# Spacing the background pieces behind the last big first-layer tile by TensorE time

## The chip, the cores and the metric

The kernel runs on one core of a Trainium2 chip. The metric is the device time of one execution in microseconds (us), the median of several runs; lower is better. The engines are TensorE (PE in the profile, PEld its weight loads), VectorE (DVE), ScalarE (ACT), GpSimd (POOL) and SyncE (SP, which issues the transfers).

## The reference

Three parts follow each other: windowed attention, a routed expert layer with a gate, and a second expert layer in which every expert takes exactly `N // E` tokens.

```
x = attention(q, k, v)                       # 3072 tokens x 512
e_idx = argmax(x @ w_gate + bias[modality])  # first layer: each token to its best expert
x = gate_w * (relu(x @ w1[e]) @ w2[e])
logits = x @ w_gate2                         # second layer: greedy, at most cap = 384 tokens for each expert
for idx in argsort(-logits.flatten()):
    tok, e = idx // E, idx % E
    if free(tok) and counts[e] < cap: assign(tok, e)
out = relu(x[assigned to e] @ w21[e]) @ w22[e]
```

The routing of the second layer needs the second gate's logits of every token, so it can begin in full only when the last tile of the first layer has been computed.

## The kernel before

The first expert layer (`moe1`) runs eight tiles through `Ffn.run`: six big ones of 512 tokens (four blocks of 128) and two small ones of 128 tokens, numbered 0 to 7 here. A tile has eight steps, and the loop has steps 0 to 69. In a step, the first part is the first matmul of one slice of weights (`ph`, L871 for a small tile, L928 for a big one), the second part is the second matmul (`y`, L871) of an earlier slice: two steps back for a big tile, six for a small one. Every matmul is done three times, with high and low parts of both operands (`w1h`, `w1l`, `w2h`, `w2l`, `hh`, `hl`); ACT rounds a slice of weights to its high part and DVE subtracts to get the low part, two steps ahead. Steps 48 to 63 make the first parts of the two small tiles; steps 50 to 53 have no second part, and steps 64 to 69 no first part. A small tile's `hr` is transposed on PE after each fourth slice.

Each step has four ticks (`side(0)` to `side(3)`: behind the first part, behind that, behind the second part's first block, at the end of the step). A tick issues a part of the weights' rounding, sometimes a transposition of the next tile's tokens (`xprep`, into the one PSUM bank `tr`), and then calls the hook, which takes pieces from the background queue `BG` in their order and issues them. The order of the instructions on each engine is thereby written out by hand: an engine works through them in that order.

When a block's second matmul is done, `yout` copies it to `yr` on ACT and adds pieces to the queue. For the last big tile and the small ones these are `put` (a store to `xs`), `turn` (four transposes on PE into `tr`, and a copy to `yt` on ACT), `logits` (four fp32 matmuls on PE into the bank `rt`) and `keep` (DVE copies the logits out; for a small tile it also prepares its part of the search). Behind the last block of the last big tile come the fifteen pieces of `Route.pre`, which prepare the search for the first expert of the second layer: b1 to b6 (bounds of the logits), v1 to v3 (best expert and comparison, DVE), p1 (13 small matmuls, PE), v4 (DVE), p2 (one matmul, PE), v5, v6, v7 (DVE). Pieces that do nothing (`nop`) stand between them; a tick takes one piece, or two when more than twelve wait. `late_ids` of the second small tile is added in step 54. What is left when the loop ends is issued by `bg.drain()`, and then `moe2` begins with the first count of its search (L1410 into `rt`).

`Clock` is a count kept while the program is built: `clk.pe` grows by 1/2400 us for each column that TensorE gets. The second layer's routing (`Route.steps`) is placed by it. In the first layer `clk.mm` is called for the matmuls and the transposes of tokens and of `hr`, but not for `turn` and `logits`.

Of the kernel before, what the change touches and what calls it, by code (L numbers as in the profile page):

```python
# [66 lines left out]
class K:  # L67
    def __init__(self):
        self.clk = Clock()
# [82 lines left out]


class BG:
    def __init__(self):
        self.q = []

    def add(self, *fs):
        self.q.extend(fs)

    def pop(self, n=1):
        for _ in range(n):
            if self.q:
                self.q.pop(0)()

    def drain(self):
        while self.q:
            self.q.pop(0)()


LST, LPV, LRO = 3, 2, 4
# [812 lines left out]
class Src:  # L984
# [15 lines left out]
    wait = 0  # L1000
# [7 lines left out]
    pop = idle  # L1008


class Src1(Src):

    wait = 12
# [29 lines left out]

    def force_e(self, j):
        while not self.ready_e(j):
            self.G.bg.pop(1)

    def force_x(self, j):
        while not self.ready_x(j):
            self.G.bg.pop(1)  # L1050

    def entry(self, w, j):
        return self.G.etab[0:1, w, j:j + 1] if j < NE else self.G.tab[0:1, w, j - NE:j - NE + 1]
# [97 lines left out]
def moe1(tc, g, G, src, rt, w1, w2, wg2, wg2T):  # L1151
    nc = tc.nc
    with ExitStack() as ctx:
        ctx.enter_context(tc.manual_schedule())
        f = Ffn(ctx, tc, g, "m1", tpe=TPE, rawpool=src.pool, vsplit=True)
        g.pst = lambda: f.ps.tile([128, 512], F32, name="rt")
        bg = G.bg
        wgb = gate_rows(nc, f, wg2T)
        wgc = f.wk.tile([128, 4, E], F32, name="wgc", bufs=1)
        nc.sync.dma_start(wgc, wg2.rearrange("(c p) e -> p c e", p=128))  # L1160
        nop = lambda: None
        bank = lambda: f.ps.tile([128, 512], F32, name="y1")
        static = list(range(SBIG)) + list(range(NE + NBIG, NE + NBIG + SSML))
        V = nc.vector

        def yout(j, a, y):
            c = src.first(j)
            late = c - NMAIN
            yr = f.wk.tile([128, DM], F32, name=f"yr{(a + max(late, 0)) % 4}", bufs=1)
            lg = rt.LG[:, c + a]  # L1170
            nc.scalar.activation(yr, y, AF.Copy, scale=src.gate(j, a))
            st = {}

            def turn():
                p = f.ps.tile([128, 512], F32, name="tr", bufs=f.trbufs)
                for c in range(4):
                    nc.tensor.transpose(p[:, 128 * c:128 * c + 128], yr[:, 128 * c:128 * c + 128], g.ident)
                st["t"] = f.wk.tile([128, 4, 128], F32, name="yt")
                nc.scalar.activation(st["t"], p, AF.Copy)
                if j == static[-1]:  # L1180
                    f.warm(WT[5])

            def logits():
                st["p"] = f.ps.tile([128, 512], F32, name="rt")[:, 0:E]
                for c in range(4):
                    nc.tensor.matmul(st["p"], st["t"][:, c, :], wgc[:, c, :], start=(c == 0), stop=(c == 3))
                if j == static[-1]:
                    f.warm(WT[6])

            def keep():  # L1190
                if late >= 0:
                    rt.keep(late, st["p"])
                V.tensor_copy(lg, st["p"])

            def put():
                nc.sync.dma_start(rt.xs[128 * (c + a):128 * (c + a) + 128, :], yr)

            if j in static[:-3]:
                bg.add(put, *dots(nc, f, yr, wgb, lg))
            else:  # L1200
                bg.add(nop, put, nop, turn, nop, nop, nop, logits, nop, keep)
                if j == static[SBIG - 1] and a == src.width(j) - 1:
                    bg.add(*rt.pre(bank, 1))

        def onx(j, xg):
            if j == static[SBIG - 1]:
                bg.add(*rt.main_ids())
            elif j in static[SBIG:]:
                bg.add(*rt.late_ids(static.index(j) - SBIG))
            if j == static[-1]:  # L1210
                nc.gpsimd.drain()

        f.run(static, w1, w2, src, yout, hook=lambda: bg.pop(2 if len(bg.q) > 12 else 1), pre=(src.raw, dict(src.xg)),
              onx=onx, LEAD=2)
        bg.drain()

# [6 lines left out]
XO = 9  # L1223
X0 = 2.0
SC = 6
PW = 4, 3, 3
WT = 7, 2, 6, 3, 6, 4, 8, 16, 0, 2
BIG = 3.0e38
BG1 = 1.0e37
# [67 lines left out]
class Route(Src):  # L1297
# [115 lines left out]
    def pre(self, bank, wait):  # L1413


        nc, g, p = self.nc, self.g, self.p
        V = nc.vector
        both, main = slice(0, 2), slice(0, HT)
        mb = bank()
        pn, pb2, pv = (self.views(mb)[i] for i in (1, 5, 6))  # L1420
        pb2 = pb2.rearrange("p (a e) -> p a e", a=2)
        bs, pd = self.bounds(V, mb, "a")
        dd0 = p.tile([128, 2, NIT], F32, name="dd0")
        gg = p.tile([JC, 2, E], BF, name="gg2")
        gs = p.tile([JC, E], F32, name="gs")
        J8 = p.tile([128, E], F32, name="J8")
        L = self.L

        def b5():
            V.tensor_scalar(self.lo0, pd[:, 1:2], -1.0, None, op0=OP.mult)  # L1430
            V.tensor_tensor(self.span, pd[:, 0:1], self.lo0, op=OP.subtract)
            self.sizes(V, pd)

        def b6():
            V.tensor_scalar(self.J, self.nrow, 4.0, None, op0=OP.mult)
            V.tensor_scalar(self.fl, g.iota[:, 0:E], 1.0, self.J, op0=OP.add, op1=OP.mult)
            self.widths(V, dd0, 0, self.span)
            V.tensor_scalar(self.lop, dd0[:, 0, 0:1], -128.0, self.lo0, op0=OP.mult, op1=OP.add)

        def v1():  # L1440
            V.tensor_copy(fold(L)[:, both, HT + 1:HR], bc(self.fl[:, None, None, :], [128, 2, HR - HT - 1, E]))
            Lm = fold(L)[:, both, main]
            V.tensor_tensor(Lm, self.LG[:, 0:NMAIN].rearrange("p (a t) e -> p a t e", a=2),
                            bc(self.pn.rearrange("p (a t) -> p a t", a=2)[:, :, :, None], [128, 2, HT, E]), op=OP.add)
            V.tensor_tensor(Lm, Lm, bc(self.fl[:, None, None, :], [128, 2, HT, E]), op=OP.max)

        def v2():
            self.best(V, both, main)

        def v3():  # L1450
            self.compare(V, both, main, dd0[:, 1, 0:1])

        def p1():
            nc.tensor.matmul(pv, g.ones, self.vb, start=True, stop=True, skip_group_check=True)
            self.count(pn, range(HT))

        def v4():
            V.tensor_copy(gs, pn[JC:2 * JC, E:2 * E])
            V.tensor_tensor(gs, pn[0:JC, 0:E], gs, op=OP.add)
            V.tensor_reduce(self.nv, pv, axis=AX.X, op=OP.add)  # L1460
            V.tensor_scalar(self.nv, self.nv, float(CAP) - 0.5 - N, None, op0=OP.add)
            V.tensor_scalar(gg[:, 0], gs, float(CAP) - 0.5, None, op0=OP.is_ge)
            V.tensor_scalar(gg[:, 1], gs, self.nv[0:JC], None, op0=OP.is_ge)

        def p2():
            nc.tensor.matmul(pb2, g.ones[0:JC, :], gg, start=True, stop=True, skip_group_check=True)

        def v5():
            d = dd0[:, 0, 0:1]
            V.max(J8, pb2[:, 0])  # L1470
            V.tensor_reduce(self.J2, pb2[:, 1], axis=AX.X, op=OP.max)
            V.tensor_scalar(self.b0, d, -1.5, self.lo0, op0=OP.mult, op1=OP.add)
            V.scalar_tensor_tensor(self.lo, J8[:, 0:1], d, self.b0, op0=OP.mult, op1=OP.add)
            V.tensor_scalar(self.lb, J8, d, self.b0, op0=OP.mult, op1=OP.add)
            V.scalar_tensor_tensor(self.hi, self.J2, d, self.b0, op0=OP.mult, op1=OP.add)
            V.tensor_tensor(self.hi, self.hi, d, op=OP.add)

        def v6():
            V.tensor_tensor(self.span, self.hi, self.lo, op=OP.subtract)
            self.widths(V, self.dd1, 1, self.span)  # L1480
            V.tensor_scalar(self.lop, self.dd1[:, 0, 1:2], -128.0, self.lo, op0=OP.mult, op1=OP.add)

        def v7():
            self.compare(V, both, main, self.dd1[:, 1, 1:2])
        nop = [lambda: None] * wait
        q = []
        for f in bs + [b5]:
            q += [f] + nop
        q.append(b6)
        for f in (v1, v2, v3, p1, v4, p2, v5):  # L1490
            q += nop * (PW[0] if f in (p1, p2) else 1) + [f]
        return q + nop * PW[1] + [v6] + nop * PW[2] + [v7]

    def digits(self, ids, o):

# [401 lines left out]
def tile_kernel(ctx, tc, qT, kT, v4, vsT, vsR, mid, wg, mbias, w1, w2, wg2, wg2T, w21, w22, cst, out):  # L1897
    nc = tc.nc
    g = K()
# [1 line left out]
    xs = tc.dram_tile([NSL + 1, DM], F32, name="xs")  # L1901
    cp = ctx.enter_context(tc.tile_pool(name="cst", bufs=1))
    load_consts(nc, g, cp, cst)
    bg = BG()
    rp = ctx.enter_context(tc.tile_pool(name="m2r", bufs=1))
    rt = Route(nc, g, rp, xs)
    with ExitStack() as c1:
        gp = c1.enter_context(tc.tile_pool(name="gate", bufs=1))
        pre = c1.enter_context(tc.tile_pool(name="pre", bufs=2))
# [51 lines left out]
```

## Time and profile before

| | us |
|---|---|
| median of three runs | 918.66 |
| the three runs | 915.5, 918.66, 920.61 |
| profiled execution, own time | 923.71 |
| its span | 922.0 |
| PE busy | 859.1 |
| DVE busy | 635.0 |
| ACT busy | 407.7 |

The profiled execution is one more run of the same program, with the profiler on; its span goes from the first to the last instruction. A busy time is the sum of an engine's instructions in that span. Times of the trace are microseconds from the start of the span. "The granted clock" is the share of full speed at which TensorE was let run.

### The profile page before, as it was taken

Reading aid. Unit: us, or ns where it says so; the run is one execution under the profiler, and the core shown is the slowest. Engines: PE = TensorE matmul, PEld = TensorE weight load, DVE = VectorE, ACT = ScalarE, POOL = GpSimd, SP = SyncE. Lnnn points to the kernel's source line nnn. Section 1 sums busy time; section 2 is a strip of 40 time slices with the busy share of each in tenths; the row PEclk is TensorE's granted clock in tenths of the full one; section 3 lists DMA queues with packets and bytes.
Section 4 is the critical chain, followed back from the end, with each engine's and each line's share of the span. In section 5 each row is a group of like instructions: output and inputs, shape, how many; then the busy total and the mean of one; then the engine's idle time right before and its main releaser. Section 6 shows DMA issues by size and latency. Waiting matters only on the chain.

```text
span 922.0 us, 15329 instructions
## 1 busy us (share of the span) xinstructions
PE 859.1 (93%) x5035; PEld 682.6 (74%) x5040; DVE 635.0 (69%) x1815; ACT 407.7 (44%) x1135; POOL 352.9 (38%) x555
## 2 busy tenths in 40 slices
PE   8789898998999999999997887989899999999996
PEld 4556666666888888888886545778788787889995
DVE  3878688866869696969783958777868676733220
ACT  3677677763343333333335514233334233334441
POOL 2785647583311010100000005536363546555561
PEclk9999899999999999999999999999999799999999
DMA  8244555376444444444344215325353425345301
GB/s 253 93 139 139 127 152 138 106 235 229 92 160 128 147 134 141 138 138 130 115 152 155 100 48 181 121 98 174 123 168 110 135 72 177 105 142 190 115 35 39
DMA packets 68944, 123.92 MB, mean 134 GB/s; under 512 B 9075, under 2 KB 21365, under 8 KB 68726
## 3 DMA queue, kind: packets, MB, share of 16 engines
q1 hardware_dynamic: 62166, 103.41, 35.3%
q0 software_dynamic: 6688, 19.43, 6.4%
q8 instruction: 42, 0.69, 0.3%
q14 instruction: 48, 0.39, 0.2%
HBM read 103.11 MB, written 19.71 MB: 133 GB/s over the span
## 4 chain that ended last, share of the span: by engine, by line
PE 70%; DVE 15%; issue 5%; ACT 5%; POOL 3%; DMA 2%; SPq 0%; POOLq 0%; ACTq 0%; DVEq 0%
PE y L871 26%; PE ph L928 26%; PE sp L296 3%; ACT P L325 3%; PE rt L1410 2%; DVE sc L150 2%; PE tr L740 2%; PE po L368 2%; PE rc L1273 1%; DVE mx L315 1%; DVE cmp L150 1%; PE pt L333 1%; PE px L403 1%; DMA vsx<-in_vsR_dram 1%; PE y L749 1%
## 5 line engine op out<-in xcount | busy, mean ns | idle before, releaser
L937 ACT ACTIVATE hh<-ph 128x384 fp32r<-128x384 f32 (+1 forms) x112 | 60.2, 537 | 269.6 <-PE ph L928 269.0
L928 PE MATMUL ph<-xh,w1h 128*128 128x384 f32 (+1 forms) x448 | 171.6, 383 | 0.0
L871 PE MATMUL y<-w2h,hh 128*128 128x512 f32 x400 | 164.7, 412 | 0.0
L928 PE MATMUL ph<-xh,w1l 128*128 128x384 f32 (+1 forms) x448 | 163.9, 366 | 0.0
L928 PE MATMUL ph<-xl,w1h 128*128 128x384 f32 (+1 forms) x448 | 162.6, 365 | 0.0
L871 PE MATMUL y<-w2l,hh 128*128 128x512 f32 x400 | 159.6, 399 | 0.0
L871 PE MATMUL y<-w2h,hl 128*128 128x512 f32 x400 | 159.5, 399 | 0.0
L938 DVE SCALAR_TENSOR_TENSOR hl<-ph,hh 128x384 fp32r<-128x384 f32 (+1 forms) x112 | 68.5, 612 | 112.9 <-ACT hh L937 112.7
L824 POOL TENSOR_TENSOR w2l<-w2r,w2h 128x512 fp32r<-128x512 f32 x64 | 89.8, 1410 | 62.1 <-ACT w2h L820 33.5
L1083 POOL DMA_INDIRECT xg<-xd,ent x26 | 30.5, 1172 | 214.0 <-PE tr L740 111.5
L1107 DVE SCALAR_TENSOR_TENSOR junk<-yr,wgb 128x512 f32<-128x512 f32 x160 | 103.4, 686 | 0.0
L928 PEld LDWEIGHTS ph<-xh,w1h 128*128 128x128 f32 x448 | 86.8, 194 | 10.4
L928 PEld LDWEIGHTS ph<-xh,w1l 128*128 128x128 f32 x448 | 86.5, 193 | 9.7
L325 ACT ACTIVATE P<-sp,mx 128x132 f32<-128x132 f32 x192 | 69.1, 367 | 54.4 <-DVE mx L315 31.8
L928 PEld LDWEIGHTS ph<-xl,w1h 128*128 128x128 f32 x448 | 86.0, 192 | 7.8
L871 PEld LDWEIGHTS y<-w2h,hl 128*128 128x128 f32 x400 | 76.7, 192 | 17.2 <-DVE hl L976 0.4
L871 PEld LDWEIGHTS y<-w2h,hh 128*128 128x128 f32 x400 | 77.2, 193 | 12.9 <-ACT hh L975 0.4
L871 PEld LDWEIGHTS y<-w2l,hh 128*128 128x128 f32 x400 | 77.1, 193 | 12.2 <-DVE w2l L824 0.3
L843 DVE TENSOR_TENSOR w1l<-w1r,w1h 128x512 fp32r<-128x512 f32 x96 | 74.3, 774 | 13.4 <-ACT w1h L838 13.4
L838 ACT ACTIVATE w1h<-w1r 128x512 fp32r<-128x512 f32 x128 | 79.7, 623 | 5.5 <-DMA w1r<-in_w_dram 3.2
L820 ACT ACTIVATE w2h<-w2r 128x512 fp32r<-128x512 f32 x128 | 79.4, 624 | 2.7 <-issue 2.5
L296 PE MATMUL sp<-kr,qs 64*128 64x260 f32 (+1 forms) x384 | 59.8, 409 | 18.8 <-ACT P L325 17.3
(343 smaller groups left out, 1442.3 us busy)
## 6 DMA issues: line engine op xcount, KB each, us to landing
w1r<-in_w_dram SPq DMA_DIRECT2D x32, 1024.0 KB, 5.4
w2r<-in_w_dram SPq DMA_DIRECT2D x32, 1024.0 KB, 6.4
xs<-yr SPq DMA_DIRECT2D x26, 256.0 KB, 6.0
kr<-in_kT_dram SPq DMA_DIRECT2D x16, 396.0 KB, 4.0
qr<-in_qT_dram SPq DMA_DIRECT2D x16, 384.0 KB, 3.3
vr<-in_v_dram SPq DMA_DIRECT2D x16, 384.0 KB, 4.5
xd<-xb SPq DMA_DIRECT2D x16, 384.0 KB, 5.7
wgb<-in_wg2T_dram SPq DMA_DIRECT2D x1, 2048.0 KB
```

The lines of the kernel that those rows point to most:

```text
L296: nc.tensor.matmul(sp[:, hd, c0:260], qs[o:o + 64, 128 * i:128 * i + 128], kr[o:o + 64, k0:k0 + 260 - c0], start=True, stop=True)
L325: nc.scalar.activation(z.P[:, n % 2, hd, :], s.sp[:, hd, 128:260], AF.Exp, bias=s.mx[:, hd:hd + 1], accum_out=z.sm[:, n % 2, hd:hd + 1])
L820: nc.scalar.activation(ch[1][c][0], r[:, q, :], AF.Copy)
L824: eng.tensor_tensor(lo, r[:, q, :], h.bitcast(F32), op=OP.subtract)
L838: nc.scalar.activation(h, v, AF.Copy)
L843: eng.tensor_tensor(lo, v, h.bitcast(F32), op=OP.subtract)
L871: nc.tensor.matmul(o, l, r, start=(first and i == 0), stop=(end and i == 2))
L928: nc.tensor.matmul(ph, wp[:, c, :], xp_[:, c, 0:NTK], start=(d == 0 and i == 0), stop=(d == 3 and i == len(cut[d]) - 1))
L937: nc.scalar.activation(hh, ph, AF.Relu)
L938: nc.vector.scalar_tensor_tensor(hl, ph, 0.0, hh.bitcast(F32), op0=OP.max, op1=OP.subtract)
L1083: self.nc.gpsimd.indirect_dma_start(out=self.xg[j][:, a, :], out_offset=None, in_=self.G.xd[0:k, :], in_offset=bass.IndirectOffsetOnAxis(a ...
L1107: nc.vector.scalar_tensor_tensor(junk, yr[:, 0:DM], 1.0, wgb[:, e, :], op0=OP.mult, op1=OP.mult, accum_out=lg[:, e:e + 1])
```

## The change

The queue's pieces may now carry a wait: a tuple `(us, piece)` is issued only when `clk.pe` has grown by at least so much since the last piece was issued. The hook tries two pieces in a tick when a tuple stands first. `drain` and the forced pops issue without regard to waits. `turn` and `logits` add their columns to the clock. The four blocks of the last big tile are interleaved: a block's `logits` is issued together with the next block's `turn`. The `nop` pieces behind that tile and in `Route.pre` are gone; the pieces carry waits in their stead.

```diff
 class BG:
-    def __init__(self):
-        self.q = []
+    def __init__(self, clk):
+        self.q, self.clk, self.last = [], clk, 0.0
...
-    def pop(self, n=1):
+    def pop(self, n=1, force=False):
         for _ in range(n):
             if self.q:
-                self.q.pop(0)()
+                f = self.q[0]
+                if isinstance(f, tuple):
+                    wait, f = f
+                    if not force and self.clk.pe < self.last + wait:
+                        return
+                self.q.pop(0)
+                f()
+                self.last = self.clk.pe
 
     def drain(self):
         while self.q:
-            self.q.pop(0)()
+            self.pop(1, True)
...
             def turn():
+                g.clk.mm(1080)
...
             def logits():
+                g.clk.mm(2100)
...
-                bg.add(nop, put, nop, turn, nop, nop, nop, logits, nop, keep)
+                bg.add((0.3, put))
+                if a > 0:
+                    prev = held.pop()
+                    bg.add((TL, prev[0]), turn, (0.4, prev[1]))
+                else:
+                    bg.add((1.0, turn))
+                held.append((logits, keep))
+                if a == src.width(j) - 1:
+                    bg.add((TL, logits), (0.4, keep))
...
-        f.run(static, w1, w2, src, yout, hook=lambda: bg.pop(2 if len(bg.q) > 12 else 1), pre=(src.raw, dict(src.xg)),
+        f.run(static, w1, w2, src, yout, hook=lambda: bg.pop(2 if len(bg.q) > 12 or bg.q and isinstance(bg.q[0], tuple) else 1), pre=(src.raw, dict(src.xg)),
...
-PW = 4, 3, 3
+TL = 1.8
...
-        q = []
-        for f in bs + [b5]:
-            q += [f] + nop
-        q.append(b6)
-        for f in (v1, v2, v3, p1, v4, p2, v5):
-            q += nop * (PW[0] if f in (p1, p2) else 1) + [f]
-        return q + nop * PW[1] + [v6] + nop * PW[2] + [v7]
+        b1, b2, b3, b4 = bs
+        return [b1, (2.0, b2), (0.5, b3), (1.6, b4), (0.5, b5), b6, (0.5, v1), (0.5, v2), (0.5, v3), (3.2, p1), (1.2, v4),
+                (2.0, p2), (0.4, v5), (0.6, v6), (0.6, v7)]
```

## Rows read from the trace of the kernel before

**Rows 1.** The page: busy time of the engines; the chain by engine.

```profile
PE 859.1 (93%) x5035; PEld 682.6 (74%) x5040; DVE 635.0 (69%) x1815; ACT 407.7 (44%) x1135; POOL 352.9 (38%) x555
...
PE 70%; DVE 15%; issue 5%; ACT 5%; POOL 3%; DMA 2%; SPq 0%; POOLq 0%; ACTq 0%; DVEq 0%
```

**Rows 2.** Windows of the loop's tail, middle, end: length; busy time; clock; DMA share; GB/s.

```profile
487.69:532.73 45.04, 35.71 (x188) 26.89 (x186) 31.37 (x96) 24.97 (x48) 0.00 (x0) 0.96 0.36 121
500.17:521.73 21.56, 15.82 (x76) 11.67 (x75) 17.32 (x61) 10.18 (x21) 0.00 (x0) 0.92 0.34 114
532.73:537.88 5.15, 4.26 (x24) 2.51 (x25) 1.12 (x6) 1.28 (x2) 0.00 (x0) 1.00 0.15 54
```

**Rows 3.** Waits from 486 to 538, TensorE's own: us, times, longest.

```profile
PE y L1410 <- DVE cmp L1404: 2.7, 1, 2.7
...
PE ph L871 <- DVE w1l L843: 1.6, 2, 1.4
...
PE rt L1186 <- ACT yt L1179: 1.4, 2, 0.7
PE y L1375 <- DVE mm L1372: 1.4, 1, 1.4
...
PE y L1382 <- DVE d L1379: 1.1, 1, 1.1
...
PE tr L972 <- ACT yt L1179: 0.7, 1, 0.7
```

**Rows 4.** Windows of 2 us around falls of the granted clock.

```profile
506.00:508.00 2.00, 2.00 (x6) 1.51 (x6) 0.58 (x4) 0.94 (x3) 0.00 (x0) 0.50 0.62 145
544.00:546.00 2.00, 1.13 (x15) 0.92 (x15) 1.07 (x3) 0.00 (x0) 0.00 (x0) 1.00 0.00 0
546.00:548.00 2.00, 2.00 (x7) 0.69 (x6) 1.61 (x11) 0.00 (x0) 0.00 (x0) 0.55 0.00 0
```

**Rows 5.** The chain of work around 485: start, us, what.

```profile
481.73 2.72 PE y L871 x12
...
488.53 0.45 PE tr L1177 x4
```

**Rows 6.** Timeline of TensorE: p1; `logits` of the last tile; the warming matmuls.

```profile
513.05 0.89 PE L1410 MATMUL y<-OH,cmp 128*128 128x16 bf16 x12 [2.67 <-DVE cmp L1404]
...
535.04 1.05 PE L1186 MATMUL rt<-wgc,yt 128*128 128x8 f32 x8
...
535.94 1.89 PE L749 MATMUL y<-wz 128*128 128x512 bf16 x8
```

**Rows 7.** Groups by line, DVE and ACT, 487.7 to 533: busy us, mean ns, idle before.

```profile
L824 DVE TENSOR_TENSOR w2l<-w2r,w2h 128x512 fp32r<-128x512 f32 x16 | 10.8, 685 | 0.0
...
L976 DVE TENSOR_TENSOR hl<-tr,hh 128x512 fp32r<-128x512 f32 x4 | 2.7, 687 | 3.2 <-ACT hh L975 3.2
...
L838 ACT ACTIVATE w1h<-w1r 128x512 fp32r<-128x512 f32 x12 | 7.5, 623 | 0.0
```

**Rows 8.** Windows of single pieces on DVE: b6+v1, v2+v3, v4, v5, v6, v7, digits, `keep`.

```profile
508.94:510.45 1.51, 1.44 (x10) 0.94 (x8) 1.41 (x9) 0.76 (x2) 0.00 (x0) 1.00 0.71 274
511.05:512.91 1.86, 0.00 (x0) 0.00 (x0) 1.79 (x5) 1.31 (x3) 0.00 (x0) 1.00 0.01 4
514.83:515.64 0.81, 0.61 (x3) 0.27 (x2) 0.74 (x6) 0.63 (x1) 0.00 (x0) 1.00 0.00 0
516.85:517.88 1.03, 1.03 (x6) 0.82 (x6) 0.96 (x9) 0.26 (x1) 0.00 (x0) 1.00 0.00 0
519.09:519.73 0.64, 0.64 (x5) 0.51 (x4) 0.57 (x5) 0.64 (x2) 0.00 (x0) 1.00 0.00 0
520.93:522.14 1.21, 1.19 (x6) 0.63 (x4) 1.21 (x4) 0.93 (x3) 0.00 (x0) 1.00 0.86 318
523.34:523.90 0.56, 0.42 (x2) 0.38 (x3) 0.56 (x8) 0.31 (x1) 0.00 (x0) 1.00 0.95 358
526.88:528.03 1.15, 1.15 (x6) 0.94 (x6) 1.05 (x7) 0.38 (x1) 0.00 (x0) 1.00 0.00 0
```

More of the change, by code (lines that the diff above doesn't have):

```diff
@@ L1045, in force_e @@
         while not self.ready_e(j):
-            self.G.bg.pop(1)
+            self.G.bg.pop(1, True)
     def force_x(self, j):
         while not self.ready_x(j):
-            self.G.bg.pop(1)
+            self.G.bg.pop(1, True)
     def entry(self, w, j):
@@ L1162, in moe1 @@
         bank = lambda: f.ps.tile([128, 512], F32, name="y1")
+        held = []
         static = list(range(SBIG)) + list(range(NE + NBIG, NE + NBIG + SSML))
@@ L1903, in tile_kernel @@
     load_consts(nc, g, cp, cst)
-    bg = BG()
+    bg = BG(g.clk)
     rp = ctx.enter_context(tc.tile_pool(name="m2r", bufs=1))
```

## The prediction

> **What bounds the kernel now.** I read the page first. PE is busy 93% of the span and carries 70% of the chain that ended last [rows 1], so what counts is time in which PE waits, and only where the change reaches. The windows over the tail of the first layer come next, from the end of the last big tile's second-layer matmuls (487.69) to the first count of the second routing (537.88) [rows 2]. The loop's steps 50 to 69 take 45.04 us and PE is busy in 35.71 of them; in the middle stretch DVE is busy 17.32 of 21.56 and the granted clock is 0.92. After the last matmul come 5.15 us up to the first count. The waits tell what PE lacked [rows 3]: 2.7 us for `cmp` of v3, 1.4 and 1.1 for `mm` and `d` of b1 and b3, 1.4 and 0.7 for `yt` of the blocks, and 1.6 for `w1l`, which stood on DVE behind the pieces of `pre`. That is 8.9 us. So the background pieces do cost time where they stand now, and about 9 us is what a better place could win at most from waits.
>
> **Where the pieces will stand.** The kernel's clock follows from its code: a small tile adds 1536 columns (0.64 us) in the first part of a step and 0.64 in the second; steps 50 to 53 have no second part, 64 to 69 no first; the transposes of `hr` add 0.43 in steps 52, 56, 60 and 64; `turn` now adds 0.45 and `logits` 0.88. Going through the ticks with the new waits gives: turn0 right behind the last big tile's matmuls (step 49), logits0 and turn1 in step 53, logits1 and turn2 in 56, logits2 and turn3 in 58, logits3 in 60, b1 in 60, b2 and b3 in 62, b4 in 64, b5 and b6 in 65, v1, v2, v3 in 66, 67, 68. p1 wants 3.2 after v3, and the loop has one step of 0.64 left. So p1, v4, p2, v5, v6, v7, the digits of tile 7's ids and all of tile 6's and tile 7's pieces fall to `bg.drain()`, behind the last matmul. Before, v7 came out in step 60, tile 6 was done in step 63, and only tile 7's `turn`, `logits` and `keep` were left. This is the heart of the forecast: the spacing is fit for the blocks, and too wide for what comes behind them.
>
> **The loop's gain.** From 45.04 us I take the 8.9 of waits [rows 3]: each `yt` now has over a step's work between `turn` and `logits`, b1 to b4 have steps between them, p1 is gone from the loop. I take 1.7 for the clock: 0.92 granted over 21.56 us is 8% lost, 1.7 us [rows 2], and the low stretch came just after b1 to b4 had made PE idle; where it fell, PE finished 6 matmuls in 2 us at 0.50 [rows 4]. I take 2.25 for PE work that leaves the loop: p1 0.89, p2 about 0.1, tile 6's `turn` 0.45 and `logits` 0.9 [rows 5, 6] (an estimate for p2, which is one small matmul). A full-speed matmul of 512 columns takes 2.72/12 = 0.227 us [rows 5], so the matmuls left are not changed.
>
> New waits I put at 5.8 us. Steps 50 to 53 hold only 0.69 us of matmuls each once the blocks are thinned out, while a slice of weights needs 0.62 on ACT and then 0.69 on DVE [rows 7]: `w1h` of step 52 stands on ACT behind three `yr` and `yt`, some 0.9 us late. In step 54 the one `tr` bank passes from turn1 to the next tile's transposes, whose `xh` stands on ACT behind `yt`, `w1h` and `w2h`: 1.1 us over four transposes. In steps 58 and 62 `hl` (0.69) stands ahead of `w1l` on DVE: 0.5 each, 0.3 elsewhere. That makes 3.3. At the end b5, b6 and v1 (1.51 for b6 and v1 [rows 8]; b5 about 0.75) stand on DVE between the last three `w2l`: from the last `hl` to the last `w2l` DVE has about 4.05 us and PE 1.6 of matmuls, so 2.5 us of wait. The bounds of this term are 0 (all hidden) and 8.9 (what the same pieces cost now); I take 5.8, since each has its producer in an in-order queue.
>
> Loop: 45.04 - 8.9 - 1.7 - 2.25 + 5.8 = 38.0, a gain of 7.0 us.
>
> **What the end costs.** Behind the last matmul nothing covers the chain: v2 and v3 still on DVE 1.4 (1.86 less the last two matmuls); p1 with its handoff 0.95 [rows 6]; v4 0.81, p2 0.2 (an estimate, as above), v5 1.03, v6 0.64, v7 1.21, digits 0.56, `keep` of tile 6 1.15 [rows 8], handoffs between the engines 0.45 (an estimate, 0.06 to 0.1 each, as from `cmp` to p1); then `logits` of tile 7, which needs the `rt` bank that tile 6's `keep` has read, and its eight warming matmuls, 0.9 + 1.9 = 2.8 up to the count [rows 6]. That is 11.2 us where 5.15 stand now: +6.05. In the loop most of these were covered by matmuls; the cover is gone. Tile 6's store moves behind too, but SP waits there only for `yr`, long ready, and the first gather out of `xs` needs the counts first. Nothing in the second layer's instructions changes, so the shift of the first count is the shift of the end.
>
> The clock takes some of it. PE had 1.13 us of work in the 2 us before it fell to half at 546 [rows 4]; in the new end it has, by the terms above, about 5.5 in 12. [...] At half speed the eight warming matmuls take 3.8 us instead of 1.9 [rows 6], and p1 and `logits` a little more, part of it under `keep`: I take +2.0, between 0 (full clock) and 4 (all of the end at half).
>
> **Sum.** -7.0 + 6.05 + 2.0 = +1.05 us. The profiled execution took 923.71 (span 922.0), 5 us above the median of 918.66, so I put the sum on the median: 919.7 us. A change under 0.5% (4.6 us) can hardly be told from none here; the three runs themselves lie 5.1 apart.
>
> **The rivals.**
> *The loop wins and the end stays warm* (faster). If ACT and DVE keep up (DVE had only 31.37 us of work in 45.04 [rows 2], and loses the 10 of `pre` from the middle), new waits shrink from 5.8 to 1.8; if the clock holds through the end, 2.0 goes: 919.7 - 6.0 = 913.7. For it: in the middle DVE was busy 17.32 of 21.56 with `pre` among it, and ACT 10.18 [rows 2]. Against: the queues are in order and the one `tr` bank is shared. Chance 0.20.
> *The clock stays at half through the first search* (slower). Place: the counts behind the first layer. If PE is granted half from the end's beginning beyond the second count, the counts (three of about p1's 0.89 [rows 6]) and the seven warming matmuls between them (7 x 0.227) take about twice as long: 2.7 + 1.6 = 4.3 on top, 924.0. It decides if the low stretch lasts beyond 8 us; the one in the middle lost 1.7 us, so it lasted some 3.4. Chance 0.17.
> *The splits set the pace* (slower, or no change). If steps 52 to 61 are bound by `w1h`, `w1l`, `w2h`, `w2l` (per step 2 x 0.62 on ACT, 2 x 0.69 on DVE) and not by the pieces, the waits come back as waits for weights. Then 5.0 less is won and the time is 924.7. Against: per step PE has 1.36 of matmuls and 0.6 of blocks. Chance 0.10.
> *The forecast*: gain in the loop, given back in the end; its own range 916.5 to 922.5. Chance 0.53.
>
> **Numbers.** Faster by over 0.5% means under 914.1: somewhat more than half of the first rival and a little of the forecast's edge, 0.15. Slower by over 0.5% means above 923.25: most of the second and third rival (0.21) and an edge of the forecast (0.06), 0.27. The rest, 0.58, lies within. The range takes in the first rival's time and the third's: 913 to 926.
>
> **What would show it.** Right: in the waits behind 488, `mm`, `d`, `cmp` and `yt` vanish as things PE waits for inside the loop; the last second-layer matmul comes some 7 us earlier; behind it p1 (L1454 and L1410 into `y`) and the DVE lines of v4 to v7 stand with PE mostly idle; the first count comes within 3 us of where it stood; the granted clock falls between the last matmul and the first count. Wrong: p1 still among the matmuls (then my walk through the ticks is wrong); waits for `w1l` and `w2l` of over 8 us in the loop; the first count over 4 us earlier or later.

## The result and the profile after

The changed kernel takes 913.77 us (median of 13 runs), the kernel before 920.61 in runs beside it: ratio 0.9904, 95% interval 0.9875 to 0.9932. The ratio is that of the fast runs, those within 1.5% of the fastest of their kernel, and not the quotient of these two medians, which is 0.9926. The changed kernel is faster by about 1%, where 919.7 us and no change were forecast; the time lies within the range of 913 to 926. The profiled execution took 908.94 us (span 907.2).

The page of the changed kernel, busy time of the engines and the chain by engine, answers to [rows 1]: TensorE's busy time is 8.7 us shorter for the same number of instructions, and the shares of the chain hardly move.

```profile
PE 850.4 (94%) x5035; PEld 674.1 (74%) x5040; DVE 635.7 (70%) x1815; ACT 406.9 (45%) x1135; POOL 353.3 (39%) x555
...
PE 70%; DVE 13%; ACT 6%; issue 6%; POOL 3%; DMA 1%; SPq 0%; POOLq 0%; ACTq 0%; DVEq 0%
```

Windows of the changed kernel (columns as in [rows 2], the busy times in the order PE, PEld, DVE, ACT, POOL): the loop from the end of the last big tile's second matmuls on, the end up to the first count, and all that follows.

```profile
483.75:519.33 35.58, 32.21 (x162) 23.03 (x160) 25.52 (x62) 23.87 (x47) 0.00 (x0) 1.00 0.44 153
519.33:531.96 12.63, 9.58 (x51) 7.17 (x52) 7.75 (x42) 1.88 (x3) 0.00 (x0) 0.59 0.06 22
531.96:907.20 375.24, 351.21 (x2104) 294.23 (x2105) 227.79 (x586) 135.23 (x302) 186.20 (x176) 0.97 0.36 124
```

The same last window of the kernel before, which the prediction did not ask for:

```profile
537.88:922.00 384.12, 356.83 (x2104) 300.18 (x2105) 228.67 (x586) 135.68 (x302) 184.77 (x176) 0.96 0.36 121
```

Against [rows 2] the loop is 9.46 us shorter (45.04 to 35.58) and the end 7.48 longer (5.15 to 12.63): 2.0 us in all. But the part behind the first count, in which PE and DVE work through the same instructions in the same order in both kernels (x2104 on PE), is 8.9 us shorter. The rest of the 14.8 between the two spans, 3.9, lies ahead of the loop, where nothing was changed either. In the trace's own time the first count comes 5.9 us earlier, which the prediction had named as a sign of being wrong.

What TensorE waited for in the loop and the end of the changed kernel, 482 to 532 (as [rows 3]):

```profile
PE y L881 <- DVE w2l L834: 1.7, 2, 1.3
PE y L1431 <- DVE cmp L1425: 1.1, 1, 1.1
PE ph L881 <- DVE w1l L853: 1.0, 3, 0.4
PE y L1487 <- DVE gg L1484: 1.0, 1, 1.0
...
PE tr L750 <- DVE xl L752: 0.5, 1, 0.5
```

`mm` and `d` are gone, `cmp` and `gg` now stand in the end, and what is left in the loop is `w2l`, `w1l` and `xl`: PE is idle for 35.58 - 32.21 = 3.4 us there, where it was 9.3 [rows 2].

TensorE's timeline behind the last matmul (start, us, what, in brackets the idle time before): p1, p2, then tile 6's and tile 7's pieces, and the first count.

```profile
519.10 0.39 PE L881 MATMUL y<-w2h,hl 128*128 128x512 f32 x1
...
520.62 0.89 PE L1431 MATMUL y<-OH,cmp 128*128 128x16 bf16 x12 [1.10 <-DVE cmp L1425]
522.49 0.17 PE L1487 MATMUL y<-gg,ones 64*128 64x16 bf16 x1 [0.99 <-DVE gg L1484]
522.59 1.11 PE L1189 MATMUL tr<-cst,yr 128*128 128x128 f32 x4
524.39 1.87 PE L1199 MATMUL rt<-wgc,yt 128*128 128x8 f32 x8 [0.69 <-ACT yt L1191]
...
530.01 1.89 PE L759 MATMUL y<-wz 128*128 128x512 bf16 x8
531.96 0.92 PE L1431 MATMUL rt<-OH,cmp 128*128 128x16 bf16 x13
```

The pieces stand where the prediction's walk put them. Transposes and logits take 2.5 and 1.8 times as long (1.11 and 1.87 for 0.45 and 1.05 [rows 5, 6]), at a clock that fell from 1.00 to 0.50 as the matmuls ended:

```profile
519.00:523.00 4.00, 1.91 (x18) 1.46 (x18) 2.66 (x12) 0.69 (x1) 0.00 (x0) 0.56 0.17 66
523.00:527.00 4.00, 3.31 (x16) 2.86 (x15) 3.72 (x23) 0.60 (x1) 0.00 (x0) 0.50 0.00 0
527.00:531.00 4.00, 3.78 (x17) 2.57 (x17) 1.32 (x8) 0.60 (x1) 0.00 (x0) 0.66 0.02 4
```

### The profile page after: what moved, and what is told of

It is laid out like the page before. It is cut to its first block, busy times and chain, and to the rows that moved or that the text cites. A ratio compares the mean times of both kernels' runs of the same rounds, so it can differ in the third digit from the quotient of the medians.

```text
span 907.2 us, 15325 instructions
## 1 busy us (share of the span) xinstructions
PE 850.4 (94%) x5035; PEld 674.1 (74%) x5040; DVE 635.7 (70%) x1815; ACT 406.9 (45%) x1135; POOL 353.3 (39%) x555
## 4 chain that ended last, share of the span: by engine, by line
PE 70%; DVE 13%; ACT 6%; issue 6%; POOL 3%; DMA 1%; SPq 0%; POOLq 0%; ACTq 0%; DVEq 0%
PE ph L938 26%; PE y L881 26%; PE sp L306 3%; ACT P L335 3%; PE rt L1431 2%; PE tr L750 2%; DVE sc L150 2%; PE po L378 2%; PE rc L1294 1%; DVE cmp L150 1%; DVE mx L325 1%; PE pt L343 1%; PE y L759 1%; PE px L413 1%; DMA vst<-in_vsT_dram 1%
## 5 line engine op out<-in xcount | busy, mean ns | idle before, releaser
L938 PE MATMUL ph<-xh,w1h 128*128 128x384 f32 (+1 forms) x448 | 168.6, 376 | 0.0
L881 PE MATMUL y<-w2h,hh 128*128 128x512 f32 x400 | 162.5, 406 | 0.0
L938 PE MATMUL ph<-xh,w1l 128*128 128x384 f32 (+1 forms) x448 | 161.6, 361 | 0.0
```

The source lines that it names most:

```text
L881: nc.tensor.matmul(o, l, r, start=(first and i == 0), stop=(end and i == 2))
L938: nc.tensor.matmul(ph, wp[:, c, :], xp_[:, c, 0:NTK], start=(d == 0 and i == 0), stop=(d == 3 and i == len(cut[d]) - 1))
```

## The experiments

Six theories are named in what follows. A: all of the gain is in the order of the work, in the loop and the end. B: it is behind the first count. C: the crowded blocks of before let TensorE's clock fall. D: the idle end at half clock pays in the second layer. P: the place of the first count against the stretches of low clock decides which of them the second layer meets. N: neither end nor place matters there.

Every kernel below left one trace. The table cuts each into what lies ahead of the loop, the loop (here from the last first matmul of the last big tile, 477.79 in the kernel before, to the last second matmul), the end up to the first count, and the second layer from there. "Low at" is how long behind the first count the next stretch at half clock begins. Lengths come from windows of these stages, in us.

| kernel | execution | ahead | loop | end | second layer | low at |
|---|---|---|---|---|---|---|
| before | 923.71 | 477.79 | 54.94 | 5.15 | 384.12 | 8.3 |
| before, b1 | 914.38 | 477.37 | 54.97 | 5.14 | 375.22 | 8.2 |
| before, b2 | 926.09 | 480.02 | 54.80 | 5.13 | 384.35 | 8.6 |
| before, b3 | 927.11 | 477.28 | 60.05 | 5.14 | 382.93 | 7.1 |
| changed | 908.94 | 473.85 | 45.48 | 12.63 | 375.24 | 8.0 |
| changed, a1 | 924.68 | 481.84 | 45.50 | 14.60 | 380.96 | 8.5 |
| changed, a2 | 914.91 | 478.07 | 45.44 | 12.44 | 377.15 | 7.8 |
| changed, a3 | 924.32 | 477.78 | 45.45 | 14.59 | 384.68 | 8.4 |
| e1 blocks only | 926.02 | 479.49 | 53.62 | 5.42 | 385.77 | 6.4 |
| e2 `pre` only | 921.00 | 473.33 | 55.74 | 6.72 | 383.51 | 7.0 |
| e3 tight | 917.28 | 477.94 | 53.11 | 5.14 | 379.41 | 6.9 |
| e4 before, kept warm | 921.01 | 473.40 | 55.47 | 5.14 | 385.30 | 8.4 |
| e5 before, long end | 928.07 | 478.69 | 54.88 | 12.80 | 380.03 | 7.6 |
| e6 changed, warm end | 918.69 | 475.46 | 45.44 | 11.26 | 384.74 | 8.2 |
| e7 before, two fillers more | 922.86 | 478.61 | 55.00 | 5.58 | 381.91 | 7.7 |
| e8 before, four more | 918.90 | 476.32 | 55.34 | 6.00 | 379.44 | 6.8 |
| e9 changed, two fewer | 919.99 | 476.19 | 45.54 | 11.81 | 384.66 | 8.1 |
| e10 e6, two more | 907.65 | 474.11 | 45.45 | 11.71 | 374.53 | 7.4 |

The stage ahead of the loop is the same in all of these kernels, and yet it takes 473.3 to 481.8 us. Its two ends, e2 and a1, differ by the granted clock, 1.00 against 0.98:

```profile
0.00:473.33 473.33, 447.87 (x2677) 341.16 (x2680) 370.00 (x1113) 242.03 (x776) 167.52 (x378) 1.00 0.48 148
```

```profile
0.00:481.84 481.84, 455.65 (x2678) 346.51 (x2680) 369.09 (x1113) 242.62 (x776) 163.64 (x378) 0.98 0.47 146
```

So a single execution's time says little about the stages that were changed.

**The two kernels again (b1, b2, b3, a1).** No edit; one execution each.

> The kernel before, unchanged, for a second trace. Stages: to the last big tile's last second-layer matmul (487.7 in the first trace), from there to the last matmul of the first layer (45.0), from there to the first count of the second routing (5.15), and the rest (384.1). Theory A (the gain of the change lies in the tail of the first layer): the two middle stages come out within 1 us of the first trace, and what differs between traces of one kernel lies in the first and the last stage, by the number of stretches at half clock. Theory B (the gain lies behind the first count): the last stage is again about 384, against some 375 in the changed kernel.

> The kernel before, unchanged, third trace. Theory C (new, from the trace of e2, which keeps before's blocks): the blocks' turn and logits, crowded into steps 50 to 54 with waits for yt, let the granted clock fall in some executions and not in others; in e2 it stayed at half from 488 to 505 and the tail took 8 to 10 us more than it would. Then before's tail (from the last big first-layer matmul on) is about 55 in executions where the clock holds and 60 or more where it falls. Theory A (the tail of before is always 55): 55 again.

> The kernel before, unchanged, fourth trace, as the third: theory C: in one or both of the two the tail is 60 us or more with a long stretch at half clock between steps 50 and 60; theory A: 55 in both.

> The changed kernel, unchanged, for a second trace. First trace: first stage 483.75, loop's tail 35.6, end 12.6, rest 375.2. Theory A: tail and end again within 1 us of 48.2 together; the rest moves with the number of half-clock stretches and can be as long as before's 384. Theory B: the rest is again within 3 us of 375.

Each kernel has executions far apart. The loop of the changed kernel always takes 45.4 to 45.5 us; its end takes 12.4 to 12.6 or 14.6; loop and end together are 57.9 to 60.1, against 59.9 to 60.1 in three traces of the kernel before. (b1's stages ahead of the first count are as theory A has them, a1's end is 2 us longer than it allowed; theory B's 384 and 375 came out in neither.) The fourth, b3, needed 65.2: its clock fell in the crowded blocks and stayed at half for some 20 us (0.50 in every window from 495 to 515), through stretches in which PE was busy 2.6 to 4 of 4 us. Windows of b3:

```profile
491.00:495.00 4.00, 2.73 (x20) 2.08 (x17) 1.37 (x3) 3.08 (x6) 0.00 (x0) 0.99 0.91 309
495.00:499.00 4.00, 3.78 (x16) 3.50 (x16) 1.89 (x3) 1.80 (x4) 0.00 (x0) 0.50 0.00 0
...
503.00:507.00 4.00, 2.58 (x8) 1.68 (x8) 1.57 (x5) 0.80 (x2) 0.00 (x0) 0.50 0.36 138
...
511.00:515.00 4.00, 4.00 (x13) 3.18 (x12) 2.90 (x17) 1.32 (x4) 0.00 (x0) 0.50 0.74 259
```

In the second layer both kernels have executions of about 375 us and of about 384. So the 8.9 us of the profiled pair are not a fixed effect of the change; if the change acts there, then by how often each occurs. Of all runs of the changed kernel 30 of 38 took 917.5 us or less, of the runs of the kernel before beside them and beside the later kernels 21 of 129.

**e1: the blocks alone.** The interleaved, spaced blocks; `Route.pre` with its old `nop` pieces.

```diff
-        return [b1, (2.0, b2), (0.5, b3), (1.6, b4), (0.5, b5), b6, ...
+        return q + nop * PW[1] + [v6] + nop * PW[2] + [v7]
```

> The four blocks are spaced and interleaved as in the changed kernel, but the fifteen pieces of pre keep the empty pieces of before instead of waits. By the kernel's ticks pre then runs from step 60 to step 66, inside the loop, and only the second small tile's pieces and the first one's logits and keep are left for behind it. Theory A: tail about 39 us (some 3 more than the changed kernel, waits for v3 and b1 come back), end 7 to 8; the stretch 46 to 47 against 48.2 changed and 50.2 before; the time 2 us under the changed kernel's, ratio to before about 0.988. Theory B (the gain comes from the long idle stretch at the end, or from what it does to the clock later): the gain of about 1% is lost, ratio 0.995 or more.

917.74 us, ratio 0.9941 (0.9905 to 0.9976). `pre` comes back into the loop, with its waits; its waits on PE from 480 on:

```profile
PE y L1432 <- DVE cmp L1426: 3.2, 1, 3.2
PE y L1404 <- DVE d L1401: 1.5, 1, 1.5
```

The loop keeps 1.3 of its 9.5 us, the end is short. The granted clock is 0.94 over its 53.62 us, though its blocks are spaced. Loop and end together, 59.0, are about what they are in the changed kernel.

**e2: the waits of `pre` alone.** The blocks with their old order and `nop` pieces.

```diff
-                bg.add((0.3, put))
...
+                bg.add(nop, put, nop, turn, nop, nop, nop, logits, nop, keep)
```

> The blocks are issued as before (each turn and logits behind each other in steps 50 to 54), and only the pieces of pre carry the new waits. By the ticks pre runs from step 54 to 68, and the first small tile's logits and keep and the second's pieces are left for behind the loop. Theory A: of the loop's gain the part of the blocks (yt: 2.1 of waits) is lost, that of pre is kept and the end is short (7 to 8 us); the stretch 45 to 47, ratio to before 0.987 to 0.992. Theory B: ratio 0.995 or more.

917.69 us, ratio 0.9961 (0.992 to 1.0003). The waits for `mm`, `d` and `cmp` are gone from the loop, but it took 55.74 us: in this trace the clock fell in the crowded blocks as in b3, and 10.0 us of the stage were lost to it (clock 0.82 over 55.74 us; what is lost to the clock is an estimate here and below, the share that was not granted times the length). A window among the blocks:

```profile
490.00:494.00 4.00, 3.25 (x13) 2.46 (x13) 0.77 (x2) 0.60 (x1) 0.00 (x0) 0.50 0.15 59
```

What goes with a clock that holds in the loop is `pre` behind it: none of the seven traces with `pre` there lost over 0.5 us in the loop (clock 0.99 or 1.00), and all eleven with `pre` inside it, e1 with its spaced blocks among them, lost 1.6 or more (0.80 to 0.97). The two that lost by far the most, b3 (0.80) and e2 (0.82), are two of the nine with crowded blocks (e4, with its fillers, counted among them; the other seven 0.94 to 0.97); the eight with blocks spaced by 1.8 have 0.94 to 1.00: too few to tell. The ratio, 0.9961, is above the 0.987 to 0.992 that theory A had; but the intervals of e1, of e2 and of the changed kernel overlap, so how much of the gain either part holds by itself is not shown by the times.

**e3: tighter waits.** `TL` 0.6 in place of 1.8, the waits of `pre` times 0.4, so that `pre` ends in the loop.

```diff
-TL = 1.8
+TL = 0.6
```

> The changed kernel with TL 0.6 instead of 1.8 and the waits of pre at 0.4 of theirs. By the ticks the blocks' logits stand in steps 51, 53, 55, 56, pre runs from 56 to 64, the first small tile's pieces in 66 to 68, and only the second's are left behind the loop. Theory C and A alike: end 5.2 instead of 12.6; waits for d and cmp come back in part: tail 50 to 53 instead of 45.5; in sum 55 to 58 against 58 to 60. Ratio to before under the changed kernel's by 0.002 to 0.004, about 0.988. If the long end is harmless or even good, the ratio is no lower than the changed kernel's.

918.5 us, ratio 0.9961 (0.993 to 0.9992): a miss. Loop and end take 58.25 us, no less than the changed kernel's 57.9 to 60.1, though the end is 5.14 again. So the long end was not the price that I took it for: what leaves it costs about as much in the loop, in waits and in clock (0.94 over the loop's 53.11 us).

**e4: the kernel before, its blocks filled.**

```diff
+                if j == static[SBIG - 1]:
+                    f.warm(4)
```

> The kernel before, with four 512-column filler matmuls added behind the transposes of each of the four blocks of the last big tile (16 matmuls of about 0.24 us, 3.8 us of TensorE work, put into gaps where TensorE waited for yt). Theory C (part of the changed kernel's gain is that the crowded, waiting blocks of the kernel before let TensorE's clock fall, for 1.6 us lost in most traces and 12 us in one): no stretch of more than 4 us at half clock between the last big first-layer matmul and the end of the second matmuls, this stage 53 to 55 us in every trace, and a time 1 to 4 us below the kernel before (ratio 0.996 to 0.999) although work was added. Rival A (only the order of the work counts, the clock there does not): the filler costs what does not fit into the waits, 0 to 2 us more (ratio 1.000 to 1.002).

918.38 us, ratio 0.9957 (0.9923 to 0.9991): 16 matmuls more, and faster, as theory C has it. Its one trace doesn't show where: the loop lost 1.7 us to the clock (0.97) like most of the kernel before, and took 55.47, over the 53 to 55 that C had. As the fillers also move the first count, theory P would do as well.

**e5: the kernel before with a long, idle end.**

```diff
+        for _ in range(24):
+            V.tensor_copy(g.wz, g.wz)
+        f.warm(1)
         bg.drain()
```

> The kernel before, with 24 dummy copies on VectorE (128x512, bf16, in place on the filler's own operand) and one filler matmul behind them, between the loop and what is drained behind it: the first count comes some 5 to 8 us later and TensorE idles meanwhile, as in the end of the changed kernel; the rest is as before. Rival N (the second layer does not care when or with what clock the first count starts): the time rises by as much as the end got longer, 5 to 8 us (ratio 1.005 to 1.009), and the stage from the first count on stays at 375 to 384 us. Theory D (an idle end at half clock brings later stretches of half clock in the second layer to fewer or cheaper places, and this is the part of the gain that the stages ahead of it don't give): the second-layer stage is 375 to 378 us and the time rises by 3 us at the most (ratio at most 1.003).

TensorE's timeline shows the wait that was put in:

```profile
540.57 0.61 PE L749 MATMUL y<-wz 128*128 128x512 bf16 x1 [6.83 <-DVE wz L1216]
```

927.32 us. The end grew by 7.65 us (12.80), the time by 3.4 us by the ratio (1.0037, 1.0000 to 1.0074, so 0 to 6.8 us). That lies between the two theories and tells them apart badly: by its middle about half of the delay was not paid at the end of the kernel, and the second layer took 380.03.

**e6: the changed kernel with a warm end.** Four filler matmuls ahead of p1, behind it, and behind each of the two last turns. **a3** is the changed kernel in the same comparison (as **a2** was in that of e3).

```diff
-        bg.drain()
+        while bg.q:
...
+            if nm == "p1":
+                fill(4)
+            bg.pop(1, True)
+            if nm in ("p1", "turn"):
+                f.warm(4)
```

> The changed kernel, with 16 filler matmuls in its end (four ahead of the first count of the drained pieces, four behind it, four behind each of the last two turns), so that TensorE's clock should not fall there; in the profiles of the changed kernel it ran at half clock for about 10 us, from the last second matmul to 2 us before the first count. If the half clock there is a plain cost: end 8 to 10 us in place of 12.5, and a time 3 to 4 us below the changed kernel of this job (ratio to the kernel before some 0.004 lower than the changed kernel's). Theory D (the low clock in the end is what pays in the second layer): the end gets shorter as well, but the second-layer stage is 382 to 384 us, and the time is not below the changed kernel's.

> The changed kernel again, with a time beside the run of before on the same chip. Theory C: ratio about 0.991 to 0.995, since the spaced blocks never let the clock fall in the loop and before does in part of its executions; tail 45.5, end 12 to 15. Theory A (the two traces tell all: 0 to 2 us): ratio 0.998.

> The changed kernel once more, for the comparison with the three others. All theories: ratio 0.987 to 0.998, tail 45.4 to 45.5 us with no clock lost in steps 50 to 60, end 12.4 to 14.6 us. Theory D: second-layer stage 375 to 378 us where no long dip fell ahead of the last tiles; rival N: anything from 375 to 384 us, as in the kernel before.

a2: 914.72 us, ratio 0.9942 (0.9901 to 0.9984). a3: 913.01, 0.9889 (0.9858 to 0.9921). e6: 919.04, 0.9967 (0.993 to 1.0003). a3's second layer, 384.68, is not the 375 to 378 that theory D had for it. With the fillers of e6 the clock did not fall in the end; its window:

```profile
520.90:532.16 11.26, 10.47 (x67) 6.11 (x67) 7.75 (x42) 1.88 (x3) 0.00 (x0) 1.00 0.07 25
```

Clock 1.00 in place of 0.59 (0.60 in a2), and an end 1.2 to 3.3 us shorter; and yet the time is not below the changed kernel's but some 6 us above a3's beside it. In e6's trace the second layer took 384.74, as theory D has it; but it took 384.68 in a3's, so these traces don't show why e6's runs are longer. Full speed in the end did not pay.

What differs in the second layer shows in windows from 135 to 200 us behind the first count: before and b1 (the same kernel), the changed kernel and a3 (the same kernel), one fence each.

```profile
672.88:737.88 65.00, 62.64 (x386) 52.84 (x385) 44.16 (x120) 21.44 (x51) 33.20 (x31) 0.89 0.39 124
```

```profile
672.48:737.48 65.00, 63.94 (x429) 53.69 (x427) 47.94 (x139) 23.61 (x55) 37.63 (x34) 1.00 0.41 139
```

```profile
666.96:731.96 65.00, 63.51 (x428) 53.28 (x426) 47.49 (x138) 23.17 (x54) 37.62 (x34) 1.00 0.40 138
```

```profile
672.82:737.82 65.00, 61.60 (x383) 51.88 (x383) 44.93 (x119) 20.68 (x48) 32.39 (x31) 0.89 0.38 125
```

The long executions have the clock at 0.89 there and get 383 to 386 TensorE instructions done, the short ones 1.00 and 428 or 429; 0.11 of 65 us is 7.2 us of the 9 between them (an estimate). The place of the first low stretch goes with the second layer's length in the table only in part: at 8.2 to 8.6 us behind the first count five rows of seven have 384.1 to 385.3 us, at 7.8 to 8.1 two rows of three have 375 to 377. The two nearest to each other, b1 at 8.2 with 375.22 and e9 at 8.1 with 384.66, stand the wrong way round. The last four kernels move the first count against the clock, by filler matmuls alone.

**e7, e8: the kernel before, two and four fillers more behind the last logits.**

```diff
-WT = 7, 2, 6, 3, 6, 4, 8, 16, 0, 2
+WT = 7, 2, 6, 3, 6, 4, 10, 16, 0, 2
```

> The kernel before, with ten in place of eight filler matmuls behind its last logits: the first count comes two fillers (0.47 us) later, nothing else changes. Theory P (where the first count falls against the stretches of low clock decides which such stretches the second layer meets): the first low stretch begins 7.6 to 8.1 us behind the first count in place of 8.1 to 8.6, the second-layer stage is 375 to 378 us, and the median falls by 4 to 8 us (ratio 0.991 to 0.996) although work was added. Rival N (the place means nothing): the time rises by 0.5 us (ratio 1.000 to 1.001) and the stage is 375 to 384 us as in the kernel before.

> The kernel before, with twelve filler matmuls there: the first count comes 0.94 us later. Theory P: the first low stretch begins 7.1 to 7.6 us behind the first count, between the places at which traces took 379 to 383 us (6.8 to 7.0) and 380 us (7.6): stage 378 to 382 us, the median 1 to 4 us below the kernel before (ratio 0.996 to 0.999), and above the run with ten. Rival N: the time rises by 0.9 us (ratio 1.001).

e7: 923.03 us, ratio 0.9991 (0.9955 to 1.0027). The low stretch came at 7.7 as theory P has it, but the second layer took 381.91: a miss, and so this place alone does not decide; the interval of the ratio takes in theory N's 1.000 to 1.001. e8: 921.28 us, 1.0002 (0.9962 to 1.0042; two of its twelve runs, at 1781 and 4184 us, are far off). Its stage, 379.44, is as P has it, but its low stretch came at 6.8 and not at 7.1 to 7.6, and its time tells nothing.

**e9: the changed kernel, two fillers fewer; e10: e6, two more.**

```diff
-WT = 7, 2, 6, 3, 6, 4, 8, 16, 0, 2
+WT = 7, 2, 6, 3, 6, 4, 6, 16, 0, 2
```

> The changed kernel, with six in place of eight filler matmuls behind its last logits: the first count comes 0.4 to 0.5 us earlier. Theory P: in most executions the first low stretch moves from 7.8 to 8.1 us behind the first count to 8.2 to 8.6, the second-layer stage rises to 381 to 385 us, and the median rises by 4 to 8 us over the changed kernel's 912 to 914 (917 to 921 us; ratio to the kernel before 0.994 to 0.999) although work was taken away. Rival N: the median falls by 0.4 us, ratio 0.988 to 0.993.

> The changed kernel with the 16 fillers in its end (its tail and end are 56.7 us against 57.9 to 60.1 of the changed kernel, but its second layer took 384.7 us), and ten in place of eight filler matmuls behind its last logits. Theory P: the first low stretch moves from 8.2 to 7.8 us behind the first count, the second-layer stage falls to 375 to 378 us, and the median to 909 to 913 us (ratio 0.985 to 0.991), below the run with the 16 fillers alone (919) by 5 to 9 us. Rival N: 0.5 us more than that run, ratio 0.994 to 1.000.

e9: 916.21 us, ratio 0.9955 (0.992 to 0.999): work was taken away, and it is no faster; it is above the changed kernel's three medians (913.01 to 914.72), by less than P had it, and its interval overlaps with theirs, so the time alone does not settle it. e10: 913.91, 0.9909 (0.9879 to 0.994): work was added, and its median is 5.1 us below e6's, the intervals just touching. The same window as above, of e9 and of e10:

```profile
668.54:733.54 65.00, 61.69 (x384) 51.99 (x383) 44.50 (x118) 20.61 (x48) 32.06 (x31) 0.89 0.38 123
```

```profile
666.27:731.27 65.00, 63.58 (x427) 53.42 (x426) 47.49 (x139) 23.17 (x54) 37.58 (x33) 1.00 0.41 138
```

Beside the changed kernel's profiled execution and e6's, the second layer with two fillers (0.47 us) fewer or more is in the other form. But a3, with all eight fillers, is in the long one too, so one trace each does not show that the fillers did it; of theory P's four forecasts, two (e9, e10) came out about right and two (e7, e8) did not. e10's lowest run, 907.65 us, is the lowest of all, but its median is not below the changed kernel's: no version here beats it for certain.

## Why the prediction was wrong

**The step that failed** is the last one of "What the end costs": "Nothing in the second layer's instructions changes, so the shift of the first count is the shift of the end." The premise holds, the conclusion does not. In the profiled pair the first count shifted by -2.0 us against the start of the loop, and the end of the kernel by 8.9 more. b1 (375.22) and a3 (384.68) show that this is not tied to the kernel: what differs is the granted clock, 0.89 or 1.00 in the windows above. With it goes the assumption that one trace of before stands for its runs: it had the second layer in the long form. How much of the median's gain comes by this way stays open.

**Where the pieces stand:** right, each of them.

**The loop's gain:** -7.0 was predicted, -9.5 measured, in every trace of the changed kernel. The term that was mis-sized is the new waits: 5.8 taken, 3.4 measured. The wait for `w1h` of step 52, put at 0.9, was 0.2; the three `w2l` at the end cost 1.7 and not 2.5. (The terms named for the work that leaves the loop add up to 2.34 and not 2.25, which changes nothing.)

**The end:** +6.05 and +2.0 for the clock were predicted, 13.2 us in all; two traces show 12.4 and 12.6, two 14.6 (in these the clock came back only behind the first count). Right in kind, and between the two in size. With the clock at 1.00, in e6 with its fillers, it took 11.26, where the sum without the clock's term has 11.2. That the clock would fall in the new end was an estimate from one fall, at 546, behind 2 us with 1.13 of work [rows 4]; in all four traces of the changed kernel it did (0.59 or 0.60 over the end), and these ends are 1.2 to 3.3 us longer than e6's, where +2.0 was taken.

**The sum** of both, +1.05, came out at -2.2 to 0.0 against the 60.1 of the kernel before. By itself that is a kernel within 0.5%, as forecast. The median moved by 6.8. What is on top of the 0 to 2.2 was not found for certain. In one of its four traces, b3, the kernel before loses far more to the clock in the loop (0.80 in place of 0.97; 5 us longer), which no trace of the changed kernel shows (1.00 in all four); how often it occurs in the timed runs is not known. And the second layer may fall into its short form more often: the runs' times would fit (30 of 38 against 21 of 129 at 917.5 or less), but the four traces of each kernel don't show it (means of 379.5 us for the changed kernel and 381.7 for the one before, with 9 us between traces of one kernel). Loop and end together have means of 59.0 and 61.3 in these traces, the stage ahead 477.9 and 478.1.

**The rivals.** The end did not stay warm (clock 0.59 or 0.60; first rival, its 913.7 is near the median for another reason), and where it did, in e6 (1.00), it did not pay. The clock was back ahead of the first count or 1.5 to 1.6 us behind it, not at half through the first search (second rival). The splits did not set the pace (third): 1.2 us for `w1h` and `w1l`, 1.7 for `w2l`.

**What stays open:** whether the kernel before is mostly in the long form and the changed one mostly in the short one, and if so why. In the changed kernel's short traces the first count follows the clock's return in the end by 2.2 and 2.4 us, so its place against the clock is much the same each time; that this is the reason was only argued. In e9 it follows by 2.1 and the second layer is long, and e7 shows that the place of the first low stretch does not decide alone.

## What to carry to other kernels

Here the granted clock fell in some executions and not in others, and a stage of unchanged instructions differed by 9 us between two executions of one kernel (before and b1: 384.12 and 375.22 us, with the clock at 0.89 and 1.00 from 135 to 200 us into the stage): take several traces of the kernel before, cut into the same stages, before a stage is counted as unchanged. Where background work makes TensorE wait, look at the clock beside the waits: in every trace with `pre` in the loop 1.6 us or more were lost to the clock there (0.80 to 0.97), in none with `pre` behind it over 0.5 (0.99 or 1.00). What serves only the next stage can run behind the loop, where here it cost no more than it did inside.

## What the runs showed of the hardware

The granted clock fell where TensorE had no gap: in the kernel before from 1.00 to 0.50 at 679.28, in the middle of matmuls that followed each other without one (the second line is its first at half clock):

```profile
679.11 0.34 PE L928 MATMUL ph<-xh,w1h 128*128 128x384 f32 x1
679.28 0.48 PE L928 MATMUL ph<-xh,w1l 128*128 128x384 f32 x1
679.56 0.53 PE L928 MATMUL ph<-xl,w1h 128*128 128x384 f32 x1
679.88 0.63 PE L871 MATMUL y<-w2h,hh 128*128 128x512 f32 x1
```

In b1, the same kernel, the same matmuls after the same small ones kept full speed (1.00 from 678.88 to 682.28):

```profile
678.46 0.33 PE L928 MATMUL ph<-xh,w1h 128*128 128x384 f32 x1
678.63 0.33 PE L928 MATMUL ph<-xh,w1l 128*128 128x384 f32 x1
678.80 0.33 PE L928 MATMUL ph<-xl,w1h 128*128 128x384 f32 x1
678.98 0.39 PE L871 MATMUL y<-w2h,hh 128*128 128x512 f32 x1
```

Ahead of both, PE was busy without a gap for more than 4 us, with many small matmuls among its work (42 and 41 instructions in 4.00 us). So TensorE's work alone didn't tell here whether the clock would fall. 47 us later, in the kernel before, PE was idle for 1.7 of 4 us beside a busy DVE (3.93 of 4 us), and the clock was down twice as long (6.90 us for 3.40); whether the first fall brought the second is not shown. Windows of the kernel before around both:

```profile
675.28:679.28 4.00, 4.00 (x42) 3.55 (x42) 1.58 (x9) 0.97 (x3) 2.58 (x3) 1.00 0.01 2
679.28:682.68 3.40, 3.40 (x10) 2.85 (x10) 3.02 (x8) 1.53 (x3) 2.79 (x3) 0.50 0.37 93
...
726.48:730.48 4.00, 2.26 (x15) 1.65 (x14) 3.93 (x6) 1.53 (x3) 3.93 (x3) 1.00 0.01 2
730.48:737.38 6.90, 6.90 (x29) 6.06 (x29) 3.35 (x11) 0.43 (x2) 0.79 (x1) 0.51 0.48 154
```

The same places behind the first count in b1, where neither fall came:

```profile
674.88:678.88 4.00, 4.00 (x41) 3.55 (x40) 1.71 (x11) 0.96 (x3) 2.83 (x3) 1.00 0.01 2
...
726.08:730.08 4.00, 4.00 (x22) 3.41 (x20) 3.43 (x7) 0.92 (x3) 3.23 (x3) 1.00 0.00 0
```

The falls inside this kernel differ from run to run: b1 and b2, two executions of the same kernel with mean clocks of 0.984 and 0.970, are 11.7 us of 914 apart (1.3%).
